# Four middle token tiles: a quarter of the first layer's row blocks as one seven-product group in PSUM banks of the layer's own pool

## The chip, the cores and the metric

The kernel runs on one NeuronCore of a Trainium2 chip. Its engines work side by side and each takes its instructions in the order in which they were issued: PE (TensorE) multiplies matrices, PEld is the loading of its weights, ACT (ScalarE) and DVE (VectorE) work element by element, POOL (GpSimd) and SP (SyncE) mostly issue DMAs. PE writes into PSUM, which has eight banks of 128 partitions by 512 float32 values; ACT and DVE read the banks and write to SBUF. The metric is the device time of one execution in microseconds (us).

## The reference

```
scores = q k^T / 8, masked: heads 0-3 the last 32 tokens, heads 4-7 every 4th of the last 128
attn   = softmax(scores);   x = attn @ v          # 8 batches x 8 heads x 576 tokens x 64
x      -> (4608 tokens, 512)
h      = max(x @ w_in, 0)                         # w_in 512 x 2048
out    = (h * h) @ w_out                          # w_out 2048 x 512
```

Inputs and output are float32 in DRAM; the kernel multiplies in bfloat16 with float32 sums.

## The kernel before

The 4608 tokens go through the two dense layers in nine tiles of 512 tokens, counted here from one. The first two are done as four half tiles, and the rest whole. A tile is 32 steps of a list (`groups`; step r of tile n is entry 32(n-1)+r). Steps 0 to 15 are the first layer: one row block of 128 of the 2048 hidden rows each, in four matmuls of 512 columns (`mm1`, line 950) that add up over the 512 features in a bank of the pool `ps_f`, which has four; ACT then writes max(., 0) to the tile `h2` (line 963, `evict`). Once some blocks are there, DVE squares them in place (`squares`, line 927) and makes two sums of them (`sums`, lines 930 and 933). Blocks are numbered U0 to U15 here. Steps 16 to 31 are the second layer. From tile 3 on it is one group of seven block products instead of eight (`g2_seven`, P1 to P7, line 1087): the 512 tokens and the 2048 hidden rows are each cut into halves, the seven products of 16 matmuls of 256 columns are added up in banks called x, y and z, and partial results are copied out by ACT ("s", "u", "z", line 1116; "21", line 1130) or added by DVE ("11", "22", "12", line 1095), while DVE also changes two operands in place between products ("3", line 1118, and "4", line 1120). The string list `BETWEEN` says what is in each step; P1a is the first half of P1's matmuls.

In tiles 8 and 9 half of the first layer is also done with seven products (`crossing`, line 1009): two groups A and B of four row blocks each, 28 matmuls of 256 columns in place of 16 of 512. Their sums of weights (`cross_w`, line 892) and of inputs (`cross_x`, line 902) are made by DVE beforehand, and banks of other pools (`ps_a`, `ps_o`, `ps_d`) hold them. The string list `FIRST` says what is in each step: "A1" to "A7" are the products, "As", "Au", "Az" ACT's copies out of a bank, "A11", "A22", "A12" DVE's additions of a bank and a copy, "A21" ACT's max out of a bank, "Ar" two max instructions of DVE (line 1023), "Aq" a square (line 1026), "q8" and "n0" the squares and sums of before.

Beside the layers runs the attention of the next batch (`natural_step`). Its program in a tile, by the step behind which each part is issued: three visits of PE, each one bundle of small matmuls at line 636 (V5 behind step 5, V17 behind 17, V24 behind 24); ACT's exponentials of scores and DVE's masks on them (lines 673 and 675: E20 at step 31, E21 at 1, E30 at 8, E31 at 10, the four E0x and E1x at 18); ACT's logarithms (lines 654, 655, 649, 650) directly behind each visit; ACT's exponential of these (line 659) and DVE's multiplication into the layer's input `xT` (lines 662 and 664), called X2 at step 6, X3 at 20, X0 at 25, X1 at 26; and DVE's and ACT's rearranging copies R (step 21) and K, Q (26 to 33). Everything of a step comes behind the step's own group, on each engine in that order; nothing is reordered later. SP issues the output's stores behind "12" and "21" and the transposing loads of q and k; POOL issues the other loads.

## Time and profile before

| | us |
|---|---|
| median of 3 runs (lowest, highest) | 289.42 (289.24, 290.15) |
| the profiled execution | 289.26 |
| its span in the profile | 287.5 |
| PE busy in the span | 280.1 |
| tile 6 (from 174.20 to 203.15) | 28.95 |

The profile lists busy time by engine, the chain of waits that ended last, groups of instructions by source line with the mean time of one, and a timeline by engine. In the timeline a row is a run of like instructions: its start, its length, the engine, the line, the operation, what it writes and reads, how often, and in brackets how long the engine had been idle and for whom it waited. Matmuls overlap in a pipeline, so a row of matmuls ends about 0.17 us after the next one has begun; what a matmul costs is read from the starts.

### The profile page before, as it was taken

Reading aid. Unit: us, or ns where it says so; the run is one execution under the profiler, and the core shown is the slowest. Engines: PE = TensorE matmul, PEld = TensorE weight load, DVE = VectorE, ACT = ScalarE, POOL = GpSimd, SP = SyncE. Lnnn points to the kernel's source line nnn. Section 1 sums busy time; section 2 is a strip of 40 time slices with the busy share of each in tenths; the row PEclk is TensorE's granted clock in tenths of the full one; section 3 lists DMA queues with packets and bytes.
Section 4 is the critical chain, followed back from the end, with each engine's and each line's share of the span. In section 5 each row is a group of like instructions: output and inputs, shape, how many; then the busy total and the mean of one; then the engine's idle time right before and its main releaser. Section 6 shows DMA issues by size and latency. Waiting matters only on the chain.

```text
span 287.5 us, 8341 instructions
## 1 busy us (share of the span) xinstructions
PE 280.1 (97%) x3381; PEld 205.4 (71%) x3381; DVE 212.7 (74%) x468; ACT 200.3 (70%) x433; POOL 129.4 (45%) x210
## 2 busy tenths in 40 slices
PE   8989999999999999999999999999999999999993
PEld 3689756968955588557865786578657887888782
DVE  2675596898877987868785879587968779856862
ACT  7788648867986877697779777977797566327420
POOL 8689964383786778567007366980000000000000
PEclk9999999999999999999999999999999999999999
DMA  7999999999999995999899999650400040013013
GB/s 98 193 174 214 207 152 230 196 156 196 149 166 169 168 121 41 194 227 127 109 156 173 202 155 248 62 37 2 147 3 2 2 149 0 0 49 99 2 37 110
DMA packets 83125, 35.35 MB, mean 123 GB/s; under 512 B 52624, under 2 KB 78480, under 8 KB 83088
## 3 DMA queue, kind: packets, MB, share of 16 engines
q0 software_dynamic: 49280, 18.43, 55.5%
q1 hardware_dynamic: 33088, 16.16, 28.1%
q8 instruction: 26, 0.43, 0.6%
q10 hardware_dynamic: 720, 0.25, 0.4%
q14 instruction: 11, 0.09, 0.1%
HBM read 37.31 MB, written 9.44 MB: 163 GB/s over the span
## 4 chain that ended last, share of the span: by engine, by line
PE 91%; DMA 5%; POOL 1%; issue 0%; DVE 0%; POOLq 0%
PE pf L950 38%; PE pf L1087 30%; PE pf L1057 10%; DMA w_in<-in_moe_w_in_dram 3%; DMA qb<-in_q_dram 2%; PE pa L1009 2%; PE po L636 2%; PE pa L636 1%; PE po L1009 1%; PE pd L1009 1%; PE pa L299 1%; PE pf L636 1%; PE pd L636 1%; PE pa L373 1%; PE po L436 1%; POOL qb L212 0%
## 5 line engine op out<-in xcount | busy, mean ns | idle before, releaser
L950 PE MATMUL pf<-xT,w_in 128*128 128x512 bf16 (+1 forms) x640 | 117.0, 337 | 0.4 <-DMA w_in<-in_moe_w_in_dram 0.4
L950 PEld LDWEIGHTS <-w_in 128*128 128x128 bf16 x640 | 70.2, 114 | 36.3 <-DMA w_in<-in_moe_w_in_dram 0.5
L963 ACT ACTIVATE h2T<-pf 128x512 bf16<-128x512 f32 x128 | 73.4, 600 | 21.4 <-PE pf L950 20.7
L1087 PEld LDWEIGHTS <-h2T 128*128 128x128 bf16 x680 | 65.1, 98 | 9.2
L1087 PE MATMUL pf<-w_out_sb,h2T 128*128 128x256 bf16 x448 | 52.9, 273 | 0.0
L498 POOL DMA_DIRECT2D vbd<-in_v_dram x80 | 43.4, 579 | 13.1 <-DMA vbd<-in_v_dram 5.4
L927 DVE TENSOR_TENSOR h2T<-h2T 128x2048 bf16<-128x2048 bf16 (+2 forms) x38 | 30.7, 828 | 4.7 <-ACT h2T L963 4.3
L1057 PE MATMUL pf<-w_out_sb,h2T 128*128 128x512 bf16 x128 | 30.8, 379 | 0.0
L1116 ACT COPY osb<-pf 128x512 f32<-128x512 f32 x22 | 12.9, 586 | 21.7 <-PE pf L1087 19.7
L662 DVE TENSOR_TENSOR xT<-po,rec 128x512 bf16<-128x512 f32 x16 | 11.0, 690 | 21.5 <-ACT rec L659 15.8
L1095 DVE TENSOR_TENSOR osb<-pf,osb 128x512 f32<-128x512 f32 (+1 forms) x22 | 14.9, 676 | 10.1 <-PE pf L1087 4.3
L212 POOL DMA_DIRECT2D qb<-in_q_dram x18 | 13.0, 725 | 16.7 <-DMA xx<-qb 14.7
L1057 PEld LDWEIGHTS <-h2T 128*128 128x128 bf16 x128 | 11.4, 98 | 10.8
L490 POOL DMA_DIRECT2D vbd<-in_v_dram x20 | 12.1, 619 | 10.4 <-DMA qb<-in_q_dram 5.4
L968 DVE TENSOR_TENSOR h2T<-h2T 128x1024 bf16<-128x1024 bf16 (+1 forms) x20 | 11.5, 585 | 6.8 <-ACT h2T L963 6.4
L673 ACT ACTIVATE pt<-pa 128x384 bf16<-128x384 f32 (+1 forms) x32 | 15.2, 499 | 1.0 <-DVE xT L664 0.4
L659 ACT ACTIVATE rec<-rec 128x576 f32<-128x576 f32 x22 | 15.0, 683 | 0.4
L233 POOL DMA_DIRECT2D vbd<-in_v_dram x16 | 10.9, 687 | 8.6 <-DMA kb<-in_k_dram 2.3
L485 POOL DMA_DIRECT2D vd<-in_v_dram x20 | 12.2, 622 | 3.8 <-DMA kb<-in_k_dram 2.5
L1087 PE MATMUL pf<-w_diff,h2T 128*128 128x256 bf16 x112 | 13.4, 273 | 0.0
L1087 PE MATMUL pf<-w_diff,s2T 128*128 128x256 bf16 x112 | 13.4, 272 | 0.0
L212 POOL DMA_DIRECT2D kb<-in_k_dram x18 | 12.8, 711 | 0.1
(190 smaller groups left out, 481.3 us busy)
## 6 DMA issues: line engine op xcount, KB each, us to landing
out_dram<-osb SPq DMA_DIRECT2D x18, 128.0 KB, 3.9
qb<-in_q_dram POOLq DMA_DIRECT2D x7, 320.0 KB, 7.2
kb<-in_k_dram POOLq DMA_DIRECT2D x7, 320.0 KB, 8.5
vd<-in_v_dram POOLq DMA_DIRECT2D x32, 64.0 KB, 6.6
w_in<-in_moe_w_in_dram POOLq DMA_DIRECT2D x4, 512.0 KB, 7.3
w_out_sb<-in_moe_w_out_dram POOLq DMA_DIRECT2D x4, 512.0 KB, 12.5
qb<-in_q_dram POOLq DMA_DIRECT2D x7, 256.0 KB, 8.0
kb<-in_k_dram POOLq DMA_DIRECT2D x7, 256.0 KB, 9.1
```

What stands on the lines that cost most here:

```text
L212: nc.gpsimd.dma_start(t[0:n, part, hs, :], src[b, hs, t0 : t0 + RES * n, :].rearrange("h (p r) d -> p h (r d)", r=RES))
L498: nc.gpsimd.dma_start(v_rows[b % 2][p0 + 16 * r : p0 + 16 * r + 16, e, :, :], v[b, 2 * e + hl, :, :].rearrange("(i m r) d -> r m i d", r=R ...
L636: nc.tensor.matmul(out, lhs, rhs, start=begin, stop=True, skip_group_check=True)
L659: nc.scalar.activation(rec[:, :], rec[:, :], ACT.Exp, scale=-1.0)
L673: nc.scalar.activation(pt, sp[b, e][g][:, 0:n], ACT.Exp, scale=SCALE)
L927: nc.vector.tensor_tensor(out=hv, in0=hv, in1=hv, op=ALU.mult)
L950: nc.tensor.matmul(to, w_in_sb[piece][:, kt, c0 : c0 + 509 : 4], rhs, start=(kt == kts[0] and x == 0), stop=(kt == kts[-1] and x == per - ...
L963: nc.scalar.activation(hv, acc[u][:, :].rearrange("p (x n) -> p x n", x=2), ACT.Relu)
L1057: nc.tensor.matmul(cur[m][:, :], h2[:, m // 2 if per == 1 else hh, HF * (f % 2) + f // 2, P * x : P * x + P], w_out_sb[:, f, :], start=(f ...
L1087: nc.tensor.matmul(bank(nm, m, cs.start)[:, m, cs], a[:, k, P * m : P * m + P], w[:, cs], start=first and k == 0 and (m == 0 or nm == "w") ...
L1095: nc.vector.tensor_tensor(out=to[:, at, cs], in0=src[:, at, cs], in1=other[:, at, cs], op=ALU.add)
L1116: nc.scalar.copy(to, bank(nm))
```

## The change

In tiles 4 to 7 the blocks U8, U9, U12 and U13 are no longer made one by one. Steps 8 to 15 become the list `MIXED`: one group C of seven products between the single blocks U10, U11, U14 and U15. The group's three banks x, y and z and the bank of U10 are the four of `ps_f`; U11 goes to the group's x bank, U14 to that of U10, U15 to z. The saved copies of the group lie in three rows of the output staging tile `osb`. The sums of weights are eight instructions of DVE, once, in tiles 3 and 4; the sums of inputs are four per tile, issued behind steps 28 and 29 of the tile ahead, and for tile 8 they move one step later. From block U8 on, the squares and sums of these tiles are as `MIXED` says. In `BETWEEN`, which tiles 3 to 7 use, P2 is split and its first half put ahead of P1's second, so that what follows comes one step later.

```diff
+PARTLY = 1536
...
+MIXED = (
+    "C1 C2 Cs C11", "U10", "C6 C5 Cu Cz", "U11", "C7 C3 C22 C12", "U14 Cr q10", "C4 C21", "U15 Cq q14 n4",
+)
 BETWEEN = (
-    "P1a", "P1b s", "P2 3 11", "P6a 4", "P6b u", "P5a", "P5b z", "P7a", "P7b 22", "P3a", "P3b 12", "P4a", "P4b 21",
-    "", "", "",
+    "P1a", "P2a", "P1b 3 s", "P2b 11 4", "P6a", "P6b u", "P5a", "P5b z", "P7a", "P7b 22", "P3a", "P3b 12", "P4a", "P4b 21",
+    "", "",
 )
...
+    o_f = [osb[:, x, :].rearrange("p (g t) -> p g t", g=2) for x in range(3)]
...
+        for k in range(2) if small else (slice(0, 2),):
+            nc.vector.tensor_tensor(out=to[:, k], in0=a[:, k], in1=b[:, k], op=op)
...
+        mixed = PARTLY <= tk0 < CROSSED
...
-                if crossed:
+                if crossed or mixed and u >= HF:
                     return
...
+            saved = dict(zip("suz", o_f if mixed else t_f[3 * z : 3 * z + 3]))
...
+                        pool, name = (ps_f, "pf") if mixed else (ps_d, "pd") if z else (ps_o, "po") if nm == "z" else (ps_a, "pa")
+                        cur[group, nm] = pool.tile([P, DM], f32, name=name)
...
         def g1_crossed(i):
-            for code in FIRST[i].split():
-                if code[0] in "AB":
+            if mixed and i < HF:
+                return g1(i)
+            for code in (MIXED[i - HF] if mixed else FIRST[i]).split():
+                if code[0] in "ABC":
                     crossing(code)
                 elif code[0] == "U":
-                    mm1(int(code[1:]), kts)
+                    u = int(code[1:])
+                    if mixed and u > 10:
+                        acc[u] = {11: cur["C", "x"], 14: acc[10], 15: cur["C", "z"]}[u]
+                    mm1(u, kts)
...
-    CROSS_W, CROSS_X = {194: "1", 196: "2", 212: "3", 213: "4"}, {219: "12", 220: "34"}
+    CROSS_W = {91: "1", 93: "2", 98: "3", 100: "4", 194: "1", 196: "2", 212: "3", 213: "4"}
+    CROSS_X = {28: "12", 29: "34"}
...
-            cross_w(code)
-        for code in CROSS_X.get(g, ""):
-            cross_x(CROSSED, code)
+            cross_w(code, g < G * PARTLY // NT + NF)
+        for code in CROSS_X.get(g % G, "") if PARTLY - NT <= NT * (g // G) < CROSSED else "":
+            cross_x(NT * (g // G + 1), code)
```

Which product goes to which bank is in the function `crossing`: y takes products 1, 6, 7 and 4, x takes 2, z takes 5 and 3. "s" is y behind C1, "u" is y behind C6, "z" is z behind C5; C11 adds x and s, C22 adds y and z behind C7, C12 adds z and u behind C3, and C21 reads y behind C4.

More of the change, by code (lines that the diff above doesn't have):

```diff
@@ L193 @@
     t1, t2, t3 = diff[:, 1], diff[:, 0], b_of[:, 0, 1]
+    v_w = vbd[0][:, 2:4, 0:8, :].rearrange("p e i c -> p e (i c)")
+    v_w = [v_w[:, e, 512 * x : 512 * x + 512].rearrange("p (k c) -> p k c", k=2) for e in range(2) for x in range(2)]
+    v_x = kbd[:, 3, 0:8, :].rearrange("p i c -> p (i c)")
+    v_x = [v_x[:, 0:512], v_x[:, 512:1024], mask_p[:, 0:512], mask_d[:, 0:512]]
+    v_x = [x.rearrange("p (k t) -> p k t", k=2) for x in v_x]
     mk_dram = nc.inline_tensor(_masks(), name="mask_patterns")
@@ L880, in combine, with cross_w @@
         nc.vector.tensor_tensor(out=to, in0=a, in1=b, op=ALU.subtract)
-    def cross_w(code: str):
-        (w11, w12), (w21, w22) = [[w_in_sb[y][:, 2 * x : 2 * x + 2, :] for x in range(2)] for y in range(2)]
-        s1, s2_, s3, s4 = (t_w[:, x] for x in range(4))
+    def cross_w(code: str, small=False):
+        w = [[w_in_sb[2 * small + y][:, 2 * x : 2 * x + 2, :] for x in range(2)] for y in range(2)]
+        s1, s2_, s3, s4 = v_w if small else [t_w[:, x] for x in range(4)]
+        if small:
+            w = [[x.rearrange("p k (c z) -> p k c z", z=4)[:, :, :, 0:2] for x in y] for y in w]
+            s1, s2_, s3, s4 = (x.rearrange("p k (c z) -> p k c z", z=2) for x in (s1, s2_, s3, s4))
+        (w11, w12), (w21, w22) = w
         to, a, b, op = {
@@ L891, in cross_w @@
         }[code]
-        nc.vector.tensor_tensor(out=to, in0=a, in1=b, op=op)
+        for k in range(2) if small else (slice(0, 2),):
+            nc.vector.tensor_tensor(out=to[:, k], in0=a[:, k], in1=b[:, k], op=op)
     def cross_x(tk0: int, code: str):
         t0 = tk0 % RING
-        (x11, x12), (x21, x22) = [
-            [xT[:, 2 * y : 2 * y + 2, t0 + HT * x : t0 + HT * x + HT] for x in range(2)] for y in range(2)
-        ]
-        t1_, t2_, t3_, t4_ = (t_x[:, x] for x in range(4))
+        begins = (0, t0) if t0 + NT > RING else (t0, t0 + HT)
+        (x11, x12), (x21, x22) = [[xT[:, 2 * y : 2 * y + 2, c0 : c0 + HT] for c0 in begins] for y in range(2)]
+        t1_, t2_, t3_, t4_ = [t_x[:, x] for x in range(4)] if tk0 >= CROSSED else v_x
         to, a, b = {"1": (t1_, x12, x11), "2": (t2_, x22, t1_), "3": (t3_, x22, x12), "4": (t4_, x21, t2_)}[code]
@@ L983, in ffn_groups @@
         hgk = h2[:, :, :, :].rearrange("p h (g k) t -> p (h g) k t", g=2)
+        t0 = tk0 % RING
+        begins = (0, t0) if over else (t0, t0 + HT)
+        x_of = [[xT[:, 2 * a : 2 * a + 2, c0 : c0 + HT] for c0 in begins] for a in range(2)]
         def crossing(code):
-            z, what = "AB".index(code[0]), code[1:]
-            def home(nm):
-                if (z, nm) not in cur:
-                    cur[z, nm] = cur[0, "x"] if (z, nm) == (1, "x") else cur[0, "z"] if (z, nm) == (1, "z") else (
-                        (ps_d if z else ps_a if nm in "xy" else ps_o).tile([P, DM], f32, name="pd" if z else "pa" if nm in "xy" else "po"))
-                return cur[z, nm][:, :].rearrange("p (g t) -> p g t", g=2)
@@ L994, in crossing @@
-            t0 = tk0 % RING
-            w = [[w_in_sb[y][:, 2 * x : 2 * x + 2, :] for x in range(2)] for y in range(2)]
-            x = [[xT[:, 2 * a : 2 * a + 2, t0 + HT * b : t0 + HT * b + HT] for b in range(2)] for a in range(2)]
-            tw, tx = [[t[:, y] for y in range(4)] for t in (t_w, t_x)]
-            saved = dict(zip("suz", t_f[3 * z : 3 * z + 3]))
-            k1, k2 = z, 2 + z
+            group, what = code[0], code[1:]
+            mixed = group == "C"
+            z = int(group == "B")
@@ new lines, in crossing @@
+            piece = 2 if mixed else 0
+            w = [[w_in_sb[piece + y][:, 2 * x : 2 * x + 2, :] for x in range(2)] for y in range(2)]
+            tw, tx = (v_w, v_x) if mixed else ([t_w[:, y] for y in range(4)], [t_x[:, y] for y in range(4)])
+            saved = dict(zip("suz", o_f if mixed else t_f[3 * z : 3 * z + 3]))
+            k1 = 2 * piece + z
+            k2 = k1 + 2
+            def home(nm):
+                if (group, nm) not in cur:
+                    if group == "B" and nm != "y":
+                        cur[group, nm] = cur["A", nm]
+                    else:
+                        pool, name = (ps_f, "pf") if mixed else (ps_d, "pd") if z else (ps_o, "po") if nm == "z" else (ps_a, "pa")
+                        cur[group, nm] = pool.tile([P, DM], f32, name=name)
+                return cur[group, nm][:, :].rearrange("p (g t) -> p g t", g=2)
@@ L1000, in crossing @@
             products = {
-                "1": ("y", w[0][0], x[0][0], True), "2": ("x", w[0][1], x[1][0], True),
-                "3": ("z", tw[3], x[1][1], False), "4": ("y", w[1][1], tx[3], False),
+                "1": ("y", w[0][0], x_of[0][0], True), "2": ("x", w[0][1], x_of[1][0], True),
+                "3": ("z", tw[3], x_of[1][1], False), "4": ("y", w[1][1], tx[3], False),
                 "5": ("z", tw[0], tx[0], True), "6": ("y", tw[1], tx[1], False), "7": ("y", tw[2], tx[2], False),
@@ L1005, in crossing @@
             if what in products:
-                nm, lhs, rhs, begins = products[what]
+                nm, lhs, rhs, fresh = products[what]
+                step = 2 if mixed and what in "3567" else 4
                 for kt in range(2):
                     for g in range(2):
+                        c0 = 2 * z + g
                         nc.tensor.matmul(
-                            home(nm)[:, g, :], lhs[:, kt, 2 * z + g : 2 * z + g + 509 : 4], rhs[:, kt, :],
-                            start=begins and kt == 0 and g == 0, stop=(kt == 1), skip_group_check=True,
+                            home(nm)[:, g, :], lhs[:, kt, c0 : c0 + 127 * step + 1 : step], rhs[:, kt, :],
+                            start=fresh and kt == 0 and g == 0, stop=(kt == 1), skip_group_check=True,
                         )
@@ L1165, in g2_seven @@
                 product(nm, a, b, first, ks)
-        if crossed:
+        if crossed or mixed:
             return [lambda i=i: g1_crossed(i) for i in range(NF)] + [lambda i=i: g2_seven(i) for i in range(NF)]
```

## The prediction

> **What bounds the kernel now.** I read the page's busy times and chain of waits first, then busy time by stage, then the timeline of tile 6.

> ```profile
> span 287.5 us, 8341 instructions
> ...
> PE 280.1 (97%) x3381; PEld 205.4 (71%) x3381; DVE 212.7 (74%) x468; ACT 200.3 (70%) x433; POOL 129.4 (45%) x210
> ...
> PE 91%; DMA 5%; POOL 1%; issue 0%; DVE 0%; POOLq 0%
> ```

> PE is the chain. The windows view of tile 6 (length; then busy PE, PEld, DVE, ACT, POOL) shows it without a gap, and three quarters of DVE's and ACT's time taken:

> ```profile
> 174.20:203.15 28.95, 28.95 (x379) 20.37 (x377) 21.76 (x47) 22.46 (x48) 17.32 (x32) 1.00 0.54 76
> ```

> So every wait put before a matmul lengthens the run in full, and every matmul taken out shortens it. What a group of seven saves is read in tile 8, which already has two; PE's timeline:

> ```profile
> 233.68 0.60 PE L1009 MATMUL pa<-kb,qb 128*128 128x256 bf16 x4
> 234.12 0.60 PE L1009 MATMUL po<-kb,qb 128*128 128x256 bf16 x4
> 234.56 1.03 PE L950 MATMUL pf<-xT,w_in 128*128 128x512 bf16 x4
> 235.42 0.60 PE L1009 MATMUL pa<-kb,qb 128*128 128x256 bf16 x4
> ```

> A product costs 0.44 us from start to start, a row block 0.86. But tile 8 has no attention beside it. Tiles 4 to 7 have, and there the order of DVE's queue matters (timeline of tile 6, all engines; steps 6 to 15 of the first layer are the 40 matmuls):

> ```profile
> 180.11 8.82 PE L950 MATMUL pf<-xT,w_in 128*128 128x512 bf16 x40
> ...
> 181.09 0.58 ACT L655 ACTIVATE rec<-pd 64x512 f32<-64x512 f32 x1
> ...
> 182.19 0.68 ACT L659 ACTIVATE rec<-rec 128x576 f32<-128x576 f32 x1
> 182.76 1.08 ACT L963 ACTIVATE h2T<-pf 128x512 bf16<-128x512 f32 x2
> 182.90 0.69 DVE L662 TENSOR_TENSOR xT<-po,rec 128x512 bf16<-128x512 f32 x1 [3.20 <-PE pf L950]
> ...
> 184.00 1.23 DVE L927 TENSOR_TENSOR h2T<-h2T 128x2048 bf16<-128x2048 bf16 x1
> ...
> 185.26 0.69 DVE L930 TENSOR_TENSOR h2T<-h2T 128x1024 bf16<-128x1024 bf16 x1
> ...
> 185.99 0.69 DVE L933 TENSOR_TENSOR s2T<-h2T 128x1024 bf16<-128x1024 bf16 x1
> ```

> DVE stands 3.2 us before X2, which starts 0.03 us after ACT's exponential (line 659) ends; that comes behind the logarithms of visit V5. Then X2, U4 to U7's squares and the first sums keep DVE until 186.6, though U7's last matmul went in at about 181.6. Today this lateness costs nothing, as PE needs none of it before the second layer.

> **The change part by part.** *Matmuls.* Four blocks (4 x 0.865 = 3.45) become seven products (7 x 0.436 = 3.05): -0.40 a tile, -1.6 in four. [...]

> *The first wait, C6 on Cs.* C6 writes y again, so ACT's copy Cs must have read it. In tile 6, U8 began at 181.87; C1, C2, U10 fill to 183.60. ACT is late from the logarithms: U7's eviction starts 182.76, so Cs runs 183.24 to 183.83 and C6 waits about 0.27. It is contained in the next wait.

> *The second wait, U11 on C11.* U11 overwrites x, so DVE's addition C11 must have read it. Without waits U11 would start 2 x 0.436 (C1, C2) + 0.865 (U10) + 2 x 0.436 (C6, C5) = 2.61 behind U8's old start, at 184.48. C11's operands are ready at 183.9, but it stands in DVE's queue behind X2, the squares and the sums: it can start 0.61 after the second sum did (as the mask does now: 186.60) and takes 0.69 (line 1020's row), to 187.29. U11 is 2.81 late. The same from the other tiles' second sums (128.13, 157.16, 214.95) against 126.56, 155.52, 213.43: 2.87, 2.94, 2.82. Sum 11.4, and 0.05 each to wake PE (ACT woke 0.04 behind matmuls): 11.6. Queued behind it on PE are all the rest of the tile. Bounds: X2 could start 0.25 sooner or later, 10.4 to 12.6.

> *The rest of the group.* From U11 at 187.3: C7 ends 188.6, C3 189.1, U14 189.9, C4 190.4, U15 191.2. C22 (0.69) ends 189.5, before C4 rewrites y; C12 190.1, just before U15 needs z. DVE's max (0.42 and 0.29, line 1023), squares (0.69, 1.22, 0.69) and sums follow till 195. P1b needs the last square at 193.6; P1a, P2a and V17 cover until 193.9. Zero taken; without that cover, up to 0.7 a tile.

> *BETWEEN.* In tiles 3 to 7 "s" now comes behind V17 and P1b. ACT's queue in the second layer of tile 6 now:

> ```profile
> 190.72 0.59 ACT L1116 COPY osb<-pf 128x512 f32<-128x512 f32 x1 [1.15 <-PE pf L1087]
> 191.40 0.93 ACT L673 ACTIVATE pt<-pa 128x448 bf16<-128x448 f32 x2
> 192.21 0.93 ACT L673 ACTIVATE pt<-pf 128x448 bf16<-128x448 f32 x2
> ...
> 195.18 0.59 ACT L1116 COPY osb<-pf 128x512 f32<-128x512 f32 x1 [0.60 <-PE pf L1087]
> 195.67 0.69 ACT L659 ACTIVATE rec<-rec 128x576 f32<-128x576 f32 x1
> ```

> "s" is over before V17 ends (191.48), the four exponentials follow at once, and "u" waits for PE and is done before X3's line 659. With V17's end at Z, the new order is: P1b to Z+0.88, "s" from Z+1.09, exponentials from Z+1.57, logarithms Z+3.33 to 4.74 (the spacings of the trace), line 659 from Z+4.77 (step 20), and "u" (now step 21) only from Z+5.35 to 5.94. P7a rewrites y, and PE is there after six half products of 0.874, at Z+5.25. It waits 0.7, in five tiles: 3.5. Bounds 0 (if ACT gains 0.7) and 0.95 each. V24 is next: it needs X3's last piece, Z+6.68, and comes at Z+6.84; zero taken, 0.5 in a tile if DVE slips.

> *Sums.* Four `cross_x` of 0.42 a tile ahead of the K and Q copies: DVE's last mask before V5 (177.60 in tile 6, V5 at 179.46) moves 1.7 later, but V24 now has one half product more behind it (0.87): 178.4, hidden. Tile 4 has in addition four small weight sums before that mask (256 elements: between a 64x128 copy, 0.20, and the 0.42 of 512; 0.28 taken, nearer the copies): 119.83 - 0.87 + 1.7 + 1.1 = 121.76 against V5 at 121.46, 0.3 lost (0 to 0.8). The other four run in the 3.2 us in which DVE stands. Tile 8's own sums, one step later but behind an earlier V24, still come before its sixth product (now 0.47 to spare, 233.21 against 233.68): zero. In tile 7 the two weight sums of tile 8 (line 892, 0.69) now stand before X3: V24 0.4 late (0 to 0.7).

> *Loads and stores.* No load moves past another. SP's stores behind "12" and "21" come one step later. The copies Cs, Cu, Cz write staging rows that the previous tile's stores read; in tile 5 these are issued from 148.46 to 153.08, behind the transposes, and land 3 to 4 us on, about when Cs (154.3) and Cz (156.2) would write. C11 starts at 157.8 anyway, which hides up to 2.9.

> DVE's work grows by 4.3 a tile (three additions 2.07, max 0.71, sums 1.68, squares -0.18) to 26 in a tile of 32: room enough, in the wrong order. ACT's is unchanged.

> **The sum,** against the profiled execution (289.26: span 287.5 and 1.8 around it): 289.26 - 1.6 + 11.6 + 3.5 + 0.3 + 0.4 = 303.5. The median shown stands 0.16 higher, inside the runs' spread; I leave 303.5.

> **The rivals.** (a) *P7 doesn't wait*, since ACT gains 0.7 somewhere: 303.5 - 3.5 = 300.0. For it: the gap is small; against: every spacing is a row. (b) *C11 doesn't bind U11*: DVE gets to it by 183.8. Left are C6's 0.27 x 4, 3.5 and 0.7: 293.0. Against: X2's wait is in each of the four tiles. (c) *Faster*: instructions are put in the order in which their operands come, so that C11 and "u" pass the attention's work; then only the -1.6 is left, 287.7. The point from which it decides is 0.4 us of waits a tile. Tile 8 speaks for it, where the groups run without a gap; the queues above, in written order throughout, against. (d) *More waits*: V24 (0.5 in the other four tiles), P1b, the small sums, all at their upper bounds: 306 to 308. (e) *The clock falls* behind each wait and the first layer's rest (3 x 0.865 + 3 x 0.436 = 3.9) runs at half rate: +15.6, 319. The trace has 4.7 us without matmuls at its end at a granted clock of 1.00, and gaps of at most 0.91 before. [...]

> **How the numbers follow.** Forecast 0.65, (a) 0.12, (b) 0.07, (c) 0.04, (d) 0.09, (e) 0.03. The range takes the forecast, (a) and (d) with the bounds: low 289.3 - 1.6 + 10.4 = 298.1, taken as 298.0; high 307.5. About 0.3% (0.9 us) is what a measurement can tell from no change. Faster 0.04 from (c), the same 0.01 at its edge, slower 0.95.

> **What would show it.** Right: a gap of PE of about 2.6 before U11 in tiles 4 to 7, ended by DVE's line 1020 addition, whose start follows the second sum at once; a gap of 0.7 before P7a in tiles 3 to 7, ended by ACT's copy; products 0.44 apart; tile 6 some 32 us long. Wrong: U11 behind C5 without a gap, or DVE's addition ahead of the squares; then (b) or (c) holds. A gap before V24 or P1b speaks for (d).

## The result and the profile after

The changed kernel takes 311.09 us (median of 6 runs, 309.85 to 311.36) beside 289.82 us for the kernel before (6 runs, 289.24 to 290.81): a ratio of 1.072, with a 95% interval of 1.069 to 1.075. The forecast was 303.5 us, and its range ended at 307.5. The profiled execution took 311.06 us, 21.8 more than that of the kernel before. Four lines of its page: span, busy times, the granted clock in 40 slices, and the engines of the chain.

```profile
span 309.2 us, 8497 instructions
...
PE 287.4 (93%) x3429; PEld 211.8 (69%) x3429; DVE 231.4 (75%) x508; ACT 199.4 (64%) x433; POOL 129.7 (42%) x210
...
PEclk9999999999999999989997999899997999999999
...
PE 78%; ACT 7%; DMA 5%; DVE 4%; POOL 2%; issue 2%; ACTq 0%; POOLq 0%
```

PE had been 91% of the chain and is now 78%. ACT and DVE have come in, as the forecast's two waits would have it. The third line is what the forecast had not: in four slices the granted clock is below nine tenths. And PE is busy 7.3 us longer than before, although its matmuls had become cheaper.

The windows view of tile 6 (length; busy PE, PEld, DVE, ACT, POOL; granted clock):

```profile
185.79:219.79 34.00, 30.72 (x390) 21.96 (x389) 26.38 (x54) 22.21 (x48) 7.37 (x14) 0.95 0.23 41
```

The tile is 34.0 us long, not the "some 32" of the forecast. 3.3 us of it are gaps of PE, and the clock column says 0.95. Two rows of PE's timeline in this tile are the waits of the forecast, the first before U11, the second before P7a:

```profile
195.81 0.71 PE L1036 MATMUL pf<-kbd,vbd 128*128 128x256 bf16 x5
199.06 1.86 PE L965 MATMUL pf<-xT,w_in 128*128 128x512 bf16 x4 [2.54 <-DVE h2T L1047]
...
213.38 1.03 PE L1119 MATMUL pf<-w_out_sb,h2T 128*128 128x256 bf16 x8 [0.62 <-ACT osb L1148]
```

What the first wait is for stands in DVE's timeline of the same stretch:

```profile
194.50 0.69 DVE L672 TENSOR_TENSOR xT<-po,rec 128x512 bf16<-128x512 f32 x1 [1.94 <-PE pf L1036]
195.11 0.46 DVE L674 TENSOR_TENSOR xT<-pa,rec 64x64 bf16<-64x64 f32 x2
195.60 1.23 DVE L942 TENSOR_TENSOR h2T<-h2T 128x2048 bf16<-128x2048 bf16 x1
196.86 0.69 DVE L945 TENSOR_TENSOR h2T<-h2T 128x1024 bf16<-128x1024 bf16 x1
197.59 0.69 DVE L948 TENSOR_TENSOR s2T<-h2T 128x1024 bf16<-128x1024 bf16 x1
198.31 0.69 DVE L1047 TENSOR_TENSOR h2T<-pf,osb 128x512 bf16<-128x512 f32 x1
```

C11 (the last row) stands behind X2, U4 to U7's squares and the first two sums, and U11 begins 0.06 us after C11 ends. This is the queue of the forecast, row for row. The second wait is in ACT's queue: the four exponentials, the logarithms and line 669's exponential go first, then the copy "u":

```profile
208.95 0.93 ACT L683 ACTIVATE pt<-pa 128x448 bf16<-128x448 f32 x2
209.75 0.95 ACT L683 ACTIVATE pt<-pf 128x448 bf16<-128x448 f32 x2
...
212.17 0.68 ACT L669 ACTIVATE rec<-rec 128x576 f32<-128x576 f32 x1
212.76 0.57 ACT L1148 COPY osb<-pf 128x512 f32<-128x512 f32 x1
```

What the forecast dismissed is shown by four windows of the changed kernel, each 3.41 us long: the one in which tile 4's gap lies, the one in which tile 6's gap lies, and the two that follow the latter.

```profile
127.42:130.83 3.41, 1.32 (x10) 0.80 (x9) 3.25 (x7) 2.64 (x6) 2.19 (x5) 1.00 1.56 207
...
195.69:199.10 3.41, 0.87 (x9) 0.64 (x7) 3.31 (x5) 2.00 (x5) 0.00 (x0) 1.00 0.00 0
199.10:202.51 3.41, 3.41 (x13) 1.78 (x13) 1.13 (x3) 0.60 (x1) 0.00 (x0) 0.50 0.02 5
202.51:205.92 3.41, 3.41 (x25) 2.43 (x24) 3.19 (x6) 1.68 (x3) 0.00 (x0) 1.00 0.00 0
```

From 199.10 to 202.51 the clock is 0.50, and PE does 13 matmuls in the time in which it does 25 right after. The same happens in tiles 4, 5 and 7, from 130.83, 164.96 and 233.23, for 3.41 us each time. The matmuls in these four stretches take 1.36, 1.55, 1.67 and 1.66 us more than at a clock of 1.00 (start to start, against 0.216 us for 512 columns and 0.109 for 256).

Where the 21.8 us went, from the starts of PE's matmuls in the two traces:

| | forecast | measured |
|---|---|---|
| 28 products in place of 16 blocks | -1.6 | -1.6 |
| C6 and U11 on the copy and on C11, tiles 4 to 7 | 11.6 | 1.2 + 10.8 |
| P7a on "u", tiles 3 to 7 | 3.5 | 3.9 |
| V5 of tile 4, V24 of tile 7 | 0.7 | 0.5 |
| half clock, tiles 4 to 7 | 0 | 6.2 |
| tile 3 begins later (88.02, not 87.12) | 0 | 0.9 |
| sum | 14.2 | 21.9 |

The profiled execution grew by 21.8. Tile 3 begins before the change has done anything on PE; over all the kernels below, its start lies between 86.88 and 89.25 us.

### The profile page after: what moved, and what is told of

Its sections match the earlier page's. It is cut to its first block, busy times and chain, and to the rows that moved or that the text cites. A ratio compares the mean times of both kernels' runs of the same rounds, so it can differ in the third digit from the quotient of the medians.

```text
span 309.2 us, 8497 instructions
## 1 busy us (share of the span) xinstructions
PE 287.4 (93%) x3429; PEld 211.8 (69%) x3429; DVE 231.4 (75%) x508; ACT 199.4 (64%) x433; POOL 129.7 (42%) x210
## 4 chain that ended last, share of the span: by engine, by line
PE 78%; ACT 7%; DMA 5%; DVE 4%; POOL 2%; issue 2%; ACTq 0%; POOLq 0%
PE pf L965 30%; PE pf L1119 22%; PE pf L1089 9%; DMA w_in<-in_moe_w_in_dram 5%; PE pf L1036 3%; ACT pt L683 2%; PE pa L1036 2%; PE po L646 2%; DVE h2T L942 2%; ACT osb L1148 2%; ACT rec L665 2%; PE pa L646 1%; PE po L1036 1%; PE pd L1036 1%; PE pa L309 1%
## 5 line engine op out<-in xcount | busy, mean ns | idle before, releaser
L965 PE MATMUL pf<-xT,w_in 128*128 128x512 bf16 (+1 forms) x576 | 109.3, 339 | 11.8 <-DVE h2T L1047 10.2
L965 PEld LDWEIGHTS <-w_in 128*128 128x128 bf16 x576 | 63.3, 114 | 40.4 <-issue 13.3
L978 ACT ACTIVATE h2T<-pf 128x512 bf16<-128x512 f32 x112 | 64.7, 600 | 39.1 <-PE pf L965 38.5
L942 DVE TENSOR_TENSOR h2T<-h2T 128x1024 bf16<-128x1024 bf16 (+2 forms) x30 | 25.9, 865 | 2.0 <-ACT h2T L978 1.5
L1089 PEld LDWEIGHTS <-h2T 128*128 128x128 bf16 x128 | 11.4, 98 | 10.8
L1047 DVE TENSOR_TENSOR h2T<-pf,osb 128x512 bf16<-128x512 f32 x12 | 8.2, 691 | 9.4 <-PE pf L1036 9.3
```

What stands on the lines that cost most here:

```text
L942: nc.vector.tensor_tensor(out=hv, in0=hv, in1=hv, op=ALU.mult)
L965: nc.tensor.matmul(to, w_in_sb[piece][:, kt, c0 : c0 + 509 : 4], rhs, start=(kt == kts[0] and x == 0), stop=(kt == kts[-1] and x == per - ...
L978: nc.scalar.activation(hv, acc[u][:, :].rearrange("p (x n) -> p x n", x=2), ACT.Relu)
L1089: nc.tensor.matmul(cur[m][:, :], h2[:, m // 2 if per == 1 else hh, HF * (f % 2) + f // 2, P * x : P * x + P], w_out_sb[:, f, :], start=(f ...
```

## The experiments

Each expectation says what theory A and its rivals make of that kernel. In short, theory A is that the waits are those of the forecast, and that what it missed is the clock, which falls when PE has been busy too little in a stretch of 3.41 us; the rivals put the missing time elsewhere. The first four kernels share one set of runs of the kernel before (median 290.13 us), the next three another (290.43 us), and the last one has its own (290.33 us).

**PE kept busy in the gap.** Ten more matmuls of 512 columns stand before U11 in tiles 4 to 7. They write the bank of U10, which U14 starts anew; nobody reads their sums.

```diff
                 elif code[0] == "U":
                     u = int(code[1:])
...
+                    if mixed and u == 11:
+                        for _ in range(10):
+                            nc.tensor.matmul(acc[10][:, :], w_in_sb[3][:, 0, 0:509:4], w_in_sb[3][:, 1, :], ...)
```

> The changed kernel with ten further matmuls of 512 columns in each of tiles 4 to 7, put between C5 and U11 and written to U10's bank, whose values U14 overwrites (about 2.2 us of the 2.7 in which PE stood there). Theory A (the granted clock falls because PE has too little to do around that gap): the clock is 1.00 throughout, U11 starts when it did, and the matmuls behind it keep 0.216 and 0.109: 6.2 us less, 304.9. Theory B (the fall has another cause, such as the banks or the products themselves): the clock falls all the same, 311. If U11's start moved later too, the gain would shrink by as much.

Measured: 304.25 us (303.96 to 304.60), ratio 1.048 (1.044 to 1.051). It computes more than the changed kernel and is 6.8 us faster. Its granted clock doesn't fall until the last 2 us, after the layers (its mean over the 302.2 us is 0.997). The granted clock in 40 slices, and PE's timeline in tile 4:

```profile
PEclk9999999999999999999999999999999999999998
...
128.08 2.32 PE L1067 MATMUL pf<-w_in 128*128 128x512 bf16 x10
130.76 1.02 PE L965 MATMUL pf<-xT,w_in 128*128 128x512 bf16 x4 [0.36 <-DVE h2T L1047]
```

The extra matmuls fill the gap but for 0.36 us, U11 still waits for the same addition, and then its four matmuls take 1.02 us, not the 1.86 of the changed kernel. C6's and P7a's waits are as before. From tile 3's start to tile 8's the kernel takes 159.59 us, the changed one 165.86: 6.3 us, against the 6.2 counted in the half clock's stretches. So the clock is what was missing, and in these tiles it fell for want of work for PE around the gap: 0.50 for 3.41 us behind each of the changed kernel's four gaps, and no such stretch with the gaps filled.

**Half as many.** The same with `range(5)`.

> As the run with ten further matmuls before U11, but with five (1.1 us of the 2.7). So far the clock fell behind each stretch of 3.41 us on one fixed grid in which PE's matmuls had 0.21 to 0.36 of the time, and stood behind one with 0.46. Theory A (the share of such a stretch decides): the shares rise to 0.5 and more, the clock stays at 1.00, 304 to 305. Rival B (a stop of more than about 1 us in one piece is enough): some 1.3 us of stop is left in each of tiles 4 to 7, the clock falls, 309 to 311.

Measured: 304.09 us (303.47 to 304.71), ratio 1.048 (1.043 to 1.053). A gap of 1.44 us stays before U11 and the clock doesn't fall (mean 0.999 over 301.7 us). The window on the same 3.41 us grid that holds the gap of tile 4:

```profile
126.95:130.36 3.41, 1.97 (x14) 1.22 (x12) 3.31 (x5) 1.97 (x5) 2.92 (x7) 1.00 1.45 197
```

PE is busy for 0.58 of it (1.97 / 3.41). The shares in this text are read from the view in this way; those in the expectation count 0.216 or 0.109 us for each matmul and are a little smaller. Half of the matmuls bring the whole gain: in these tiles a fall either came for a whole 3.41 us or didn't come.

**The second layer in its old order.** The changed kernel with the `BETWEEN` of before.

```diff
-    "P1a", "P2a", "P1b 3 s", "P2b 11 4", "P6a", "P6b u", "P5a", "P5b z", "P7a", "P7b 22", "P3a", "P3b 12", "P4a", "P4b 21",
-    "", "",
+    "P1a", "P1b s", "P2 3 11", "P6a 4", "P6b u", "P5a", "P5b z", "P7a", "P7b 22", "P3a", "P3b 12", "P4a", "P4b 21",
+    "", "", "",
```

> The changed kernel with the list BETWEEN as it was before. Theory A (P7a waited since u stood behind the exponentials in ACT's queue): the 0.78 ahead of P7a is gone in five tiles, -3.9; but P1b now follows P1a at once and needs DVE's last squares: 0.5 to 1.0 more in four tiles; 309 to 310. Rival B (P7a waited because the group had pushed ACT's and DVE's work later, and the order of the products has no part in it): P7a still waits, 311 to 315.

Measured: 308.08 us (305.96 to 310.38), ratio 1.061 (1.054 to 1.068), a little under the 309 to 310 that theory A gave. P7a's wait is gone. In its place P1b waits 0.38, 0.47, 0.43 and 0.43 us in tiles 4 to 7 for "Cq", the group's last square, which the two half products in front of it had covered. V5 is late as well, by 0.43, 0.17 and 0.27 us in tiles 4 to 6 against 0.21 in tile 4 alone in the changed kernel, while V24 of tile 7 isn't late any more. So with this group the new order costs 4.2 (P7a 3.9, V24 0.3) and saves 2.4 (P1b 1.7, V5 0.7). The gaps before U11 are 2.70 us in all four tiles, as in the changed kernel; but the clock falls in three tiles, not in four. The windows on the grid, in tiles 5 and 6:

```profile
162.80:166.21 3.41, 1.56 (x11) 1.07 (x11) 2.33 (x6) 0.98 (x3) 1.13 (x2) 1.00 1.46 197
193.52:196.93 3.41, 0.87 (x9) 0.64 (x8) 3.31 (x5) 2.03 (x5) 3.41 (x8) 1.00 0.56 35
```

In tile 5 the gap lies across two windows of the grid. The emptier has PE busy for 0.46, and no fall follows. In tile 6 it lies within one (0.26), and from 196.93 the clock is half. The gap is as long both times, so its length alone didn't decide here. How many falls a run gets can then differ: of this kernel's four runs, the longest (310.38) has the lowest mean clock, 0.974, the shortest (305.96) the highest, 0.988, and the two between 0.983.

**The order alone.** The kernel before, with the new `BETWEEN` and nothing else.

> The kernel before with only the new list BETWEEN; no group, no sums. Theory A: the order alone makes P7a wait 0.75 to 0.79 in each of five tiles: 289.8 + 3.9 = 293.7, with nothing in the first layer. Rival B (the wait comes from the group's work): no wait, 289.8. Clock 1.00 in both.

Measured: 294.63 us (294.21 to 295.43), ratio 1.015 (1.011 to 1.019). The waits view, idle time, times, longest:

```profile
PE pf L1087 <- ACT osb L1116: 2.9, 5, 0.6
```

Start to start, P7a is 0.75 us late in each of the five tiles, 3.7 in all (the view leaves out the 0.17 us in which the last matmul drains). This term of the forecast is a price of the order, independent of the group. So is V24's in tile 7: it is 0.28 us late here without any group, and on time in the kernel with the group and the old order.

**DVE's queue put right.** The changed kernel, with the squares of U4 to U7 issued behind C12 and the first sums behind the last square.

```diff
-    ... "C7 C3 C22 C12", "U14 Cr q10", "C4 C21", "U15 Cq q14 n4",
+    ... "C7 C3 C22 C12 q4", "U14 Cr q10", "C4 C21", "U15 Cq q14 n0 n4",
```

> The changed kernel, but DVE's square of U4 to U7 is issued behind C12 and the first sums behind the last square, so that C11 stands behind X2 alone. Theory A (C11 was late because of the queue ahead of it): U11 waits at most 0.3, C6's 0.3 stays, and the clock stays at 1.00: -10.8 and -6.2; DVE's work comes back as later waits of 1 to 2 us a tile, at V24 behind X3: 298 to 302. Rival B (C11 was late for another reason, its own bank or its copy): U11 still waits over 2 us, 310 or more.

Measured: 299.75 us (299.34 to 301.22), ratio 1.033 (1.028 to 1.038). U11 doesn't wait any more and the clock doesn't fall (mean 1.000 over 298.2 us): C11 was late because of what stood in front of it. But DVE's work has only moved. It now ends later, and the waits view shows who pays:

```profile
PE po L646 <- DVE xT L672: 3.7, 4, 1.4
PE pf L1121 <- ACT osb L1150: 1.4, 5, 0.6
...
PE pf L1121 <- DVE s2T L948: 1.0, 4, 0.2
```

V24 waits for X3, which is behind the late squares and sums, and P6 for a sum; P7a's wait is shorter, since what stands before it is later. The clock stays at 1.00.

**What to do about P7a.** The kernel before with the new `BETWEEN`, and with two of the four exponentials of step 18 issued one step sooner, ahead of "s".

```diff
-        expo(0, t + 18, t + 18)
+        steps.extend((t + 17, 3, b, f"E0{x}") for x in range(2))
```

> The kernel before with only the new list BETWEEN, and with the exponentials E00 and E01 issued directly behind visit V17 instead of behind s. Theory A (P7a waits for u, which is late because s holds up all four exponentials on ACT): u comes 0.8 sooner, the wait of 0.75 in five tiles is gone or under 0.1, at most 0.3 returns at V24; 290.0 to 291.5. Rival B (P7a waits for something else, such as DVE's change of its operand): 294.6 as with BETWEEN alone.

Measured: 290.20 us (289.47 to 292.24), ratio 1.001 (0.998 to 1.004). ACT's timeline in tile 6: two exponentials, "s", then the two others.

```profile
191.71 0.93 ACT L673 ACTIVATE pt<-pa 128x448 bf16<-128x448 f32 x2 [1.82 <-PE pa L636]
192.88 0.59 ACT L1116 COPY osb<-pf 128x512 f32<-128x512 f32 x1 [0.24 <-PE pf L1087]
193.36 0.93 ACT L673 ACTIVATE pt<-pf 128x448 bf16<-128x448 f32 x2
```

In the order alone, ACT stood idle for P1b between V17 and "s" (part of the 2.99 us of its idle time before "s" in tile 6). The two exponentials now use that time, "u" is ready before P7a, and the 4.5 us of the kernel above are gone.

**A version: the group early.** With that repair, the group can go where DVE has room. Products C1 and C2 come behind U2, so that C11, C22 and C12 are done before X2; X2 comes one step later; U4, U5 and U6 take the group's x bank, U3's bank and the group's z bank; the sums of weights are issued at other steps.

```diff
 MIXED = (
-    "C1 C2 Cs C11", "U10", "C6 C5 Cu Cz", "U11", "C7 C3 C22 C12", "U14 Cr q10", "C4 C21", "U15 Cq q14 n4",
+    "U0", "U1", "U2", "C1 C2 Cs C11", "U3 q0-4", "C6 C5 Cu Cz", "U4", "C7 C3 C22 C12", "U5 q4-6", "C4 C21",
+    "U6 Cr", "U7 q6-8", "U10 Cq", "U11 q10-12 n0", "U14 q14-15", "U15 q15-16 n4",
 )
...
+    kept = const.tile([P, DM], f32, name="kept")
...
-            saved = dict(zip("suz", o_f if mixed else t_f[3 * z : 3 * z + 3]))
+            saved = dict(zip("suz", (k_f if tk0 >= 4 * NT else o_f) if mixed else t_f[3 * z : 3 * z + 3]))
...
-        norm(2, second)
+        norm(2, second, 1 if early else 2)
```

Here `k_f` is `kept` and two free pieces of a staging tile of k, which tile 4 can't have yet: there the saved copies stay in `osb`.

> The changed kernel with the group C moved to steps 3 to 9 of the first layer, where DVE stood for 3.2 us before, X2 one step later (behind C12), the squares split accordingly, E00 and E01 directly behind V17, the saved copies outside osb from tile 5 on, and the weight sums at other steps (65 in place of 91 and 93; 213 and 214 for tile 8). Theory A (all that the change lost was waits for DVE and ACT in the order of their queues, and the clock behind them): no wait in tiles 4 to 7 above 0.3, clock 1.00, 288.3 to 290, about 1.6 less than before at best. Rival B (DVE, with 4.3 us more a tile, cannot keep up in any order): 1 to 2 us of waits a tile remain, 292 to 297.

Measured: 293.59 us (290.86 to 294.87), ratio 1.011 (1.007 to 1.015). This lies in the range of rival B, but not for B's reason alone, and theory A's "no wait above 0.3" didn't hold either. In tiles 5 and 6 one matmul of the first layer waits for a DVE addition of the group, 0.50 and 0.18 us, and tile 7 runs without a wait. Tile 4 has a new and longer one. ACT's timeline there, and PE's:

```profile
124.50 0.58 ACT L1059 COPY osb<-pf 128x512 f32<-128x512 f32 x1 [2.90 <-DMA out_dram<-osb]
```

```profile
125.14 1.43 PE L1054 MATMUL pf<-kbd,vbd 128*128 128x256 bf16 x8 [2.44 <-ACT osb L1059]
```

Cs writes a row of the output's staging tile from which the store of tile 3's output still reads, and C6 stands behind it. In the changed kernel the group came 5.5 us later in the tile, and its Cs didn't wait for the store. The clock fell behind this gap too: the window of 3.41 us that holds it has PE busy for 0.97 us, a share of 0.28, and in the next one the granted clock is 0.51.

The profiled execution has another fall, long before the group, in the kernel's opening part. The window ahead of it and the window of the fall:

```profile
13.00:16.41 3.41, 1.89 (x46) 1.42 (x45) 2.60 (x7) 2.78 (x6) 1.53 (x3) 1.00 1.44 191
16.41:19.82 3.41, 3.41 (x38) 2.39 (x37) 1.01 (x3) 1.02 (x3) 3.37 (x5) 0.50 1.56 179
```

PE was busy for 0.55 of the first, more than the 0.46 behind which the clock stood in the old order. 38 of its 46 matmuls are small ones on 64 rows and 64 columns; the large ones alone, up to 13.34 and from 15.72 on, cover 0.30 of it. So the share of busy time alone doesn't part the windows ahead of a fall from the others.

**The group in three tiles.** The same without the group in tile 4 (`PARTLY = 2048`), where X2 is at its old step.

```diff
-PARTLY = 1536
+PARTLY = 2048
...
-        norm(2, second, 1 if early else 2)
+        norm(2, second, 2 if b > 4 else 1)
```

> The early group of v1_group_early in tiles five to seven alone; tile four computes its sixteen blocks as before the change, so no saved copy goes to an output row whose store is under way. Theory A (what v1_group_early lost was the one wait of 2.6 us in tile four and the fall of the clock behind it; tiles five to seven gain by their own): no wait of over 0.5 us in tiles four to seven beyond those of the kernel before, no half rate in them, tile five to seven some 0.2 to 0.4 us shorter each than the 28.95 us of before, and 288.7 to 289.7 us beside a kernel before of 290.4 (ratio 0.994 to 0.9975). Rival B (the copies and sums of the group and the second step of delay of X2 cost as much as three products of 3.05 us save): 290.0 to 290.8, ratio 0.9985 to 1.0015. Rival C (the group in the early steps fills the ACT queue, so that a visit or a copy waits in each tile, and the clock falls in at least one stretch): above 291.5, ratio over 1.004.

Measured: 289.24 us (12 runs, 288.43 to 289.85) beside 290.33 (17 runs, 289.42 to 292.08), ratio 0.9954 (0.9933 to 0.9975): 1.1 us faster than the kernel before, half a per cent, and its clock doesn't fall before the layers end (mean 0.999 over 288.1 us, less than 1 us at half rate in all). DVE's timeline in tile 5, where C11 is followed by the squares, C22, C12 and only then X2; below it tile 6 in the windows view:

```profile
152.31 0.69 DVE L1065 TENSOR_TENSOR h2T<-pf,kb 128x512 bf16<-128x512 f32 x1
152.92 1.22 DVE L960 TENSOR_TENSOR h2T<-h2T 128x2048 bf16<-128x2048 bf16 x1
154.62 0.69 DVE L1065 TENSOR_TENSOR h2T<-pf,kept 128x512 bf16<-128x512 f32 x1 [0.49 <-ACT rec L683]
...
155.82 0.68 DVE L690 TENSOR_TENSOR xT<-po,rec 128x512 bf16<-128x512 f32 x1
```

```profile
175.64:204.33 28.69, 28.60 (x390) 21.54 (x389) 25.78 (x56) 22.28 (x48) 18.45 (x34) 1.00 0.69 89
```

Tiles 5 to 7 take 28.70, 28.69 and 28.44 us, against 28.96, 28.96 and 28.78 before: 0.26, 0.27 and 0.34 saved, of the 0.40 that seven products in place of four blocks are worth. Theory A of this run holds. What the other 0.06 to 0.14 us a tile go to isn't settled.

## Why the prediction was wrong, step by step

- *Matmuls, -1.6: right.* Products stand 0.44 us apart and blocks 0.86 at a granted clock of 1.00 (109 ns for a matmul of 256 columns, 216 for one of 512), and the last version gains by it.
- *U11 on C11, 11.6 with C6's wait contained: right in mechanism and size.* Measured 2.70 to 2.71 us before U11 and 0.28 to 0.33 before C6 in each tile, 12.0 together. Moving the squares out of the way removed the wait of U11, as it had to; C6's stayed.
- *P7a on "u", 3.5: right.* 0.75 to 0.79 us each, 3.9 together, inside the bounds; the order alone shows 3.7.
- *Tile 4's V5 and tile 7's V24, 0.3 and 0.4: right in size,* 0.21 and 0.26. The reason given for V24 was wrong: of tile 8's two weight sums one stood before X3 already in the kernel before (at 225.33, X3 at 225.94), the other stands behind it in both, and the order alone makes V24 0.28 late. The rest of the group at zero held too, but by the cover that the forecast named: without the two half products in front, P1b waits 0.4 us a tile for the last square.
- *The clock, which the sum put at nothing, is the step that failed.* Rival (e) had the right mechanism, and it was given 0.03. Two things in it were wrong. First the ground for that: it held against the fall that the trace of before has gaps "of at most 0.91" and 4.7 us without matmuls at its end, at a granted clock of 1.00, and so went by the length of a gap. The runs show that gaps of 2.7 us do it, and that one of the same length didn't, so that a length was the wrong thing to compare; none of them shows a length from which on the clock falls. The gaps of at most 0.91 couldn't tell, for none came near 2.7. Nor could the 4.7 us at its end: the changed kernel ends in the same way, its last row of matmuls is over at 304.57, and its clock falls only at 308.32, where a stretch of the grid ends. In the trace of before the record of the clock has its first fall at 287.78, just past the end of the span at 287.5. Second the price: (e) let all that was left of the first layer run at half rate, 3.9 us a tile. The half clock lasted 3.41 us, in tile 4 the first 0.6 us of it still in the gap, and cost 1.4 to 1.7 a tile: 6.2, not 15.6. With a fall behind each of the four gaps before U11, at the measured price, the forecast's own sum would have been 309.7; the tile's later start and the other terms make up the rest to 311.06.
- *Rivals (a) to (d)* didn't hold: P7a waited, C11 bound, nothing passed the attention's work, and V24 and P1b took no more than was counted.

## What to carry to other kernels

A wait put before PE had two prices here: the time itself (2.7 us before U11), and the clock behind it (a further 1.4 to 1.7 us, where the gap left PE busy for 0.25 to 0.39 of a 3.41 us stretch); look for both in the trace, and where a gap can't be avoided, fill it (five or ten matmuls that nobody reads, in each of four tiles, gave back some 7 us here). A cheaper operation that adds copies and additions to busy queues paid here only where its additions are issued ahead of the long in-place work of the same engine, and where its buffers are free: at the end of the first layer, in four tiles and with the new order's waits, it cost 7%; at the start, in three tiles and with ACT's order repaired, it gained 0.5%. When a step is moved, look at what each engine stands idle for at that place; two exponentials issued in ACT's idle time undid a wait of 0.75 us in five tiles.
